# One weight load put behind four transposing DMAs, and twenty score products issued more than once, in a fused attention and MLP kernel

## Chip, cores and metric

The kernel runs on one core of a Trainium2 chip, as one launch. The metric is the device time of one execution in microseconds (us), from the median of the runs shown. Beside the timed runs stands one execution recorded by the hardware profiler.

## What is computed

The inputs are bf16: `x` of 2048 rows by 640, `wqkv` (640 x 1920), `wo` (640 x 640), and for the second branch `w1`, `w2` (640 x 640), `w3` (640 x 1536), `w4` (1536 x 640).

```python
def _A_ref(x, wqkv, wo):            # B=1, S=2048, D=640, H=32, Dh=20
    qkv = (x @ wqkv).reshape(B, S, 3, H, Dh).transpose(2, 0, 3, 1, 4)
    q, k, v = qkv[0], qkv[1], qkv[2]
    scores = jnp.einsum("bhqd,bhkd->bhqk", q, k) * (Dh ** -0.5)
    p = _softmax(scores, axis=-1)
    o = jnp.einsum("bhqk,bhkd->bhqd", p, v)
    return o.transpose(0, 2, 1, 3).reshape(B, S, D) @ wo

def _B_ref(x, w1, w2, w3, w4):
    h = _gelu(_layernorm(x) @ w1)
    # g0..g3: the four column quarters of h, shifted by +1, -1, +2, -2 rows
    x1 = x + jnp.concatenate([g0, g1, g2, g3], axis=-1) @ w2
    return x1 + _gelu(_layernorm(x1) @ w3) @ w4

xn = _layernorm(x)
return x + _A_ref(xn, wqkv, wo) * _silu(_B_ref(xn, w1, w2, w3, w4))
```

## The kernel before

The program is a list of tasks (`Task`), each with an engine, a function that issues its instructions, and the atoms it reads and writes. `Planner.follow` takes the tasks in the order of `TABLE`, a string in which each task stands as two characters (followed by one character for each buffer choice). This one order, written out, fixes the order on every engine and on SP's DMA queue; semaphores are derived from the atoms. An engine never overtakes its own order. A DMA task waits on SP for what it reads, and everything behind it on that queue waits with it.

**Prologue.** `load_inputs` brings `x` in eight loads. LayerNorm makes `xn`; `ln1_and_transpose` makes its transpose `xnT`, needed by all projections, in four groups `g` of 512 columns. Groups 0, 1 and 3 go through TensorE (transposes, line 1054) with evictions by VectorE (line 1065) or ScalarE (line 1062). Group 2 (`TD = (2,)`) goes through four transposing DMAs on SP, `tx_8` to `tx_11`, one for each 128 rows (line 1043). `prep` then makes the keys and queries of the first four heads: `KT_c` and `QT_c` are products of chunk `c` of `xnT` (`mm_tile`, line 708, five steps of four products each), so `KT_2` reads what the four DMAs write. Scores against the first keys and their exponentials begin while later key chunks are still being made.

In the SP order before, the load of W1 (`ld_w1`, lines 1937 and 1938, 640 x 640 bf16) stands after `tx_9` and before `tx_8`, `tx_10`, `tx_11`. Next behind these stands the copy of queries into `QM` (line 1365). W1 is first used by `b_w1`, which also multiplies by rows `RR` that SP loads later.

**Attention.** 32 heads in 8 quads of 4, each with 4 chunks `qc` of 512 queries and 16 key tiles `kt` of 128 keys. `score_pair(b, qc, kt, a, ...)` issues the products of two of the four heads (`a` = 0 or 1) for one key tile, into two PSUM banks. In one form (line 1594, `score`) it is two products, each on 32 rows of the array, 32 x 128 by 512 columns; the two pairs `a` use different rows. In the other (line 1607) it is eight products of 128 x 32. Which one is taken depends on the neighbours in the TensorE order (`mode`, set in `follow`). ScalarE takes the exponential of most pairs (`exp_act`, line 1654, 128 x 1024 in one instruction). For some pairs VectorE makes them from integer arithmetic instead: `score_both` (line 1685), then `block_bits` (line 1573 on VectorE, line 1571 on GpSimd). The products with V are lines 1407 and 1585.

**The second branch** is woven into the same order: `b_w1`, `b_w2`, `b_w3`, `b_w4` fill TensorE between scores; the last of it, the steps that end in line 2093 (tanh) and 2102, is done early in quad 7. After each chunk of quad 7, `finish_qc` multiplies with `wo` and stores.

Of the kernel before, what the change touches and what calls it, by code (L numbers as in the profile page):

```python
# [16 lines left out]


class Task:
    __slots__ = ("part", "flex", "id", "eng", "dur", "fn", "reads", "writes", "due", "name",  # L20
                 "preds", "succs", "order_preds", "start", "finish", "seq",
                 "signals", "dma_sem", "lat", "pos", "npred", "prio", "is_dma",
                 "acq", "rel", "stream", "sidx", "cls", "nbytes", "mode", "ndma", "tile", "dlat", "lock")
# [34 lines left out]
class Planner:  # L58
# [87 lines left out]
            self.buf_atoms[name].add(atom)  # L146

    def task(self, eng, dur, fn, reads=(), writes=(), due=None, name="", lat=0.0,
             is_dma=False, acq=None, rel=None, stream=None, after=(), cls=0, nbytes=0, mode=0, ndma=1, tile=None, dlat=0.0, lock=False, part=0, flex=False):
        tid = len(self.tasks)  # L150
        t = Task(tid, eng, dur, fn, tuple(reads), tuple(writes), due, name, lat, is_dma)
        t.cls = cls
        t.nbytes = nbytes
        t.mode = mode
        t.ndma = ndma
        t.tile = tile
        t.part = part or 3 * mode
        t.flex = flex
        t.dlat = dlat
        t.lock = lock or eng == "pool"  # L160
        if is_dma and nbytes:
            t.lat = self.dma_lat0 + nbytes / self.dma_bw + dlat
        t.acq = [acq] if isinstance(acq, tuple) else list(acq or ())
        t.rel = rel
        self.tasks.append(t)
        preds = set()
        opreds = set()
        for bn in after:
            preds.update(self.buf_inherit.get(bn, ()))
        if stream is not None:  # L170
            assert is_dma
            lst = self.streams.setdefault(stream, [])
            t.stream = stream
            t.sidx = ndma + (self.tasks[lst[-1]].sidx if lst else 0)
            if lst:
                preds.add(lst[-1])
            lst.append(tid)

        def add(p, atom):
            if p == tid:  # L180
                return
            pt = self.tasks[p]
            if (pt.eng == "pe" and eng == "pe" and atom in self.pe_psum_atoms
                    and not pt.is_dma):
                opreds.add(p)
            else:
                preds.add(p)

        for a in t.reads:
            own = self.atom_owner.get(a)  # L190
            if a in self.last_writer:
                add(self.last_writer[a], a)
            elif own is not None:
                for p in self.buf_inherit.get(own, ()):
                    add(p, a)
        for a in t.writes:
            own = self.atom_owner.get(a)
            seen = False
            if a in self.last_writer:
                add(self.last_writer[a], a)  # L200
                seen = True
            for r in self.readers.get(a, ()):
                add(r, a)
                seen = True
            if not seen and own is not None:
                for p in self.buf_inherit.get(own, ()):
                    add(p, a)
        for a in t.reads:
            self.readers[a].append(tid)
        for a in t.writes:  # L210
            self.last_writer[a] = tid
            self.readers[a] = []
        opreds -= preds
        t.preds = preds
        t.order_preds = opreds
        return t

    def follow(self, table):
# [19 lines left out]
        while at < len(table):  # L238
            t = tasks[len(code) * code[table[at]] + code[table[at + 1]]]
# [5 lines left out]
        while at < len(table):  # L245
            t = tasks[len(code) * code[table[at]] + code[table[at + 1]]]
            at += 2
            e = t.eng
            if e == "pe":
                nx = next(later)  # L250
                if t.flex and (pe_mode or (nx is not None and (nx.mode or nx.flex))):
                    t.mode, t.dur = 1, self.row_dur
            st = eng_free[e]
            if t.lock and e == "pool" and held_by is not None and held_by not in t.preds:
                t.preds.add(held_by)
# [217 lines left out]
class Cfg:  # L473
# [5 lines left out]
    def __init__(self, S=2048, D=640, H=32, F=1536):  # L479
# [93 lines left out]
        self.W7 = (0, 1)  # L573
        self.LAST = [[[4, 2]], [[3, 2]]]
        self.HP = True
        self.EARLY = 4
        self.PP |= {(quad, qc, 0, 2) for quad in range(8) for qc in range(4)}
        self.PP |= {(0, 0, 1, 3), (0, 0, 1, 2)}
# [59 lines left out]
class Gen:  # L638
# [29 lines left out]
    def A(self, name, *key):  # L668
        a = (name,) + key
        self.pl.own(name, a)  # L670
        return a
# [924 lines left out]
    def score_pair(self, b, qc, kt, a, hs, sa, gb):  # L1596
        T, A = self.T, self.A
        me = []
        early = self.tag == "0_0" and kt < self.cfg.EARLY
        def fn(e):  # L1600
            for jj in range(2):
                out = self.bank(hs[jj].slot if isinstance(hs, tuple) else hs.slots[jj])
                if me[0].mode:
                    ins = self.score(e, out[:, :], b, qc, kt, 2 * a + jj, early)
                    continue
                for c in range(4):
                    ins = e.matmul(out[32 * c:32 * c + 32, :], self.KT[:, b, 128 * kt + 32 * c:128 * kt + 32 * c + 32],  # L1607
                                   self.QM[:, gb, 2 * a + jj, :], start=True, stop=True, tile_position=(0, 32 * c))
            return ins
        me.append(T("pe", 220 if gb is None else 440, fn,  # L1610
                    reads=[A("KT", b, kt // 4)] + ([A("QE")] if early else [A("QT", b, qc), A("QTa", b, qc)]) + ([] if gb is None else [A("QM", gb)]),
                    writes=[sa], name=f"sc{self.tag}_{kt}_{a}", mode=int(gb is None), part=a + 1, flex=gb is not None, cls=-1,
                    acq=("S2",) + hs if isinstance(hs, tuple) else ("S", hs)))

    def score_act(self, b, qc, kt, a, gb=None):
# [289 lines left out]
    def b_alloc1(self):  # L1905

        cfg = self.cfg
        T, A = self.T, self.A
        S, D, KC, NT = cfg.S, cfg.D, cfg.KC, cfg.NT
# [24 lines left out]
          reads=[A("T16", 0), A("T16", 1)], writes=[("dq",)], is_dma=True, nbytes=8192, name="rr0", ndma=3)  # L1934
        self.RR = self.alloc("RR", [6, 512], FP32)
        W1 = self.W1 = self.alloc("W1", [KC, D], BF16)
        T("sp", C_SP, lambda e: e.dma_start(W1[:, :, :], self.aps["B_w1"].rearrange("(kc p) n -> p kc n", p=128)),
          writes=[A("W1")], is_dma=True, nbytes=KC * 128 * D * 2, name="ld_w1")
        W2 = self.W2 = self.alloc("W2", [KC, D], BF16)
        T("sp", C_SP, lambda e: e.dma_start(W2[:, :, :], self.aps["B_w2"].rearrange("(kc p) n -> p kc n", p=128)),  # L1940
          writes=[A("W2")], is_dma=True, nbytes=KC * 128 * D * 2, name="ld_w2")
# [171 lines left out]
    r"<%K&=&>%T&%O'%Z%[%P%Q$o'2(K%L*>$&?(T(L%U*<%M%t%V%W%]%_(%`%a%b%R%^'+#0&t%X%F%H%S%I&#)&$%c%N&%*3'*?#&&&'&*(&+&((M*4(*@)&,&-&.&/'?%'@'A'B'C&)&L$&C#&1*0#&2&6)&M&"  # L2113
# [115 lines left out]
```

## Time and profile before

| | |
|---|---|
| time, median of 3 runs | 797.91 us (797.26 to 798.15) |
| the profiled execution's own time | 799.57 us |
| its span, first to last instruction | 797.8 us |
| mean granted TensorE clock | 0.991 |
| busy: TensorE, ScalarE, VectorE, GpSimd | 774.4, 766.1, 688.1, 441.4 us |

In the profile PE is TensorE (PEld its weight loads), ACT ScalarE, DVE VectorE, POOL GpSimd, SP the engine that issues the DMAs. A row of the timeline has start, duration, engine, line, operation, what it writes and reads, how many instructions were merged, and in brackets the idle time before it and what ended it. Starts and ends of neighbouring instructions overlap, since the engines are pipelined. A row of the windows has the stretch, its length, and for each engine the busy time and the number of instructions, then the granted clock as a share of full speed, the DMA engines' mean busy share and their GB/s.

### The profile page before, as it was taken

How to read it: one execution, taken by the hardware profiler on the slowest of the kernel's cores; microseconds unless marked ns; L12 is line 12 of the kernel's file. 1: busy time of each engine (PE TensorE's matmuls, PEld its weight loads, DVE VectorE, ACT ScalarE, POOL GpSimd, SP SyncE). 2: the span in 40 equal slices, each digit the busy share in tenths (PEclk: the TensorE clock that was granted, in tenths of full speed). 3: DMA queues.
4: the chain of work that ended last, by engine and by line, in shares of the span. 5: the costliest groups of instructions: out<-in, count | busy, mean ns of one | idle time of the engine just before them, and what ended most of it. 6: DMA issues, size and time to landing. Idle time of an engine off the chain costs nothing.

```text
span 797.8 us, 29573 instructions
## 1 busy us (share of the span) xinstructions
PE 774.4 (97%) x13392; PEld 321.2 (40%) x13392; DVE 688.1 (86%) x914; ACT 766.1 (96%) x798; POOL 441.4 (55%) x238
## 2 busy tenths in 40 slices
PE   8899999999999999999999999999999999999996
PEld 5433333334444433333534444334334344433464
DVE  8788889989999999989998889898978888786876
ACT  7799999999999999999999999999999999998986
POOL 6476646552546647665653655756264464735832
PEclk9999999999999999999999999999999999997998
DMA  6421452342131322333241132324333113123353
GB/s 173 71 72 46 111 134 52 90 107 48 37 86 35 54 65 58 70 78 65 79 100 47 26 81 52 85 44 87 53 93 44 43 35 85 22 51 103 78 157 101
DMA packets 141357, 58.22 MB, mean 73 GB/s; under 512 B 113728, under 2 KB 136432, under 8 KB 141232
## 3 DMA queue, kind: packets, MB, share of 16 engines
q1 hardware_dynamic: 141232, 56.33, 31.2%
q8 instruction: 105, 1.72, 0.9%
q14 instruction: 20, 0.16, 0.1%
HBM read 34.70 MB, written 10.33 MB: 56 GB/s over the span
## 4 chain that ended last, share of the span: by engine, by line
ACT 54%; PE 36%; DVE 5%; DMA 3%; POOL 1%; issue 0%; SPq 0%; DVEq 0%
ACT arena L1654 47%; PE psum L708 13%; PE psum L1594 8%; PE psum L1585 6%; PE psum L1407 4%; PE psum L1607 4%; ACT arena L2065 3%; DVE arena L1685 2%; ACT arena L1636 1%; DMA arena<-arena 1%; ACT arena L1973 1%; ACT arena L2093 1%; DVE arena L1573 1%; PE psum L1464 1%; PE psum L1438 1%; POOL arena L1881 1%
## 5 line engine op out<-in xcount | busy, mean ns | idle before, releaser
L1654 ACT ACTIVATE arena<-psum 128x1024 bf16<-128x1024 f32 x726 | 678.3, 1038 | 18.7 <-PE psum L1594 14.0
L1571 POOL TENSOR_TENSOR arena<-arena 128x2048 int32<-128x2048 int32 x92 | 330.1, 3598 | 224.0 <-DVE arena L1573 104.4
L1685 DVE TENSOR_SCALAR arena<-psum 128x1024 uint16<-128x1024 f32 x268 | 326.3, 1220 | 55.1 <-PE psum L1594 49.8
L708 PE MATMUL psum<-arena 128*32 128x320 bf16 (+1 forms) x5808 | 336.0, 332 | 1.9 <-DMA arena<-arena 1.2
L1594 PE MATMUL psum<-arena 32*128 32x512 bf16 x1606 | 195.5, 387 | 10.7 <-ACT arena L1654 6.6
L708 PEld LDWEIGHTS psum<-arena 128*32 128x32 bf16 x5808 | 143.2, 96 | 122.0 <-issue 31.5
L1585 PE MATMUL psum<-arena 128*22 128x512 bf16 x2144 | 188.1, 383 | 0.0
L1407 PE MATMUL psum<-arena 128*22 128x512 bf16 x1448 | 137.8, 384 | 0.3
L1573 DVE TENSOR_SCALAR arena<-arena 128x4096 uint16<-128x4096 uint16 (+1 forms) x127 | 133.2, 1072 | 2.5 <-PE psum L1585 1.8
L1594 PEld LDWEIGHTS psum<-arena 32*128 32x128 bf16 x1606 | 53.6, 91 | 177.8 <-ACT arena L1654 97.7
L1607 PE MATMUL psum<-arena 128*32 128x512 bf16 x1512 | 114.9, 381 | 0.3
L1585 PEld LDWEIGHTS psum<-arena 128*22 128x22 bf16 x2144 | 52.5, 91 | 62.1 <-issue 26.1
L1720 POOL TENSOR_TENSOR arena<-arena 128x512 bf16<-128x512 f32 x30 | 40.8, 1360 | 27.1 <-DVE arena L1573 20.0
L1407 PEld LDWEIGHTS psum<-arena 128*22 128x22 bf16 x1448 | 35.7, 91 | 47.8 <-issue 22.8
L1607 PEld LDWEIGHTS psum<-arena 128*32 128x32 bf16 x1512 | 31.6, 95 | 40.9 <-ACT arena L1654 30.2
L2058 DVE CAST arena<-psum 128x512 bf16<-128x512 f32 x48 | 32.7, 682 | 4.5 <-PE psum L708 4.3
L1274 DVE CAST arena<-psum 128x512 bf16<-128x512 f32 x40 | 27.3, 687 | 8.2 <-PE psum L708 8.0
L1881 POOL TENSOR_TENSOR arena<-arena 128x640 bf16<-128x640 bf16 x12 | 16.7, 1398 | 23.4 <-DVE arena L1573 8.8
L919 DVE BATCH_NORM_STATS2 arena<-arena 128x6 f32<-128x320 bf16 x54 | 24.9, 482 | 0.6 <-DMA arena<-in_A_x_dram 0.5
L1636 ACT ACTIVATE arena<-psum 128x2048 bf16<-128x2048 f32 x13 | 24.7, 1897 | 0.7 <-PE psum L1594 0.7
L1819 DVE SCALAR_TENSOR_TENSOR arena<-psum,arena 128x320 bf16<-128x320 f32 x32 | 15.3, 484 | 11.1 <-PE psum L708 10.9
L1707 DVE STREAM_TRANSPOSE arena<-psum 128x512 f32<-128x512 f32 x30 | 21.3, 710 | 1.9 <-PE psum L1585 1.3
(133 smaller groups left out, 342.7 us busy)
## 6 DMA issues: line engine op xcount, KB each, us to landing
arena<-in_B_w_dram SPq DMA_DIRECT2D x48, 160.0 KB, 2.7
arena<-arena SPq DMA_DIRECT2D x124, 32.0 KB, 2.1
arena<-in_B_w_dram SPq DMA_DIRECT2D x4, 960.0 KB
arena<-in_A_x_dram SPq DMA_DIRECT2D x8, 320.0 KB, 5.7
arena<-in_A_x_dram SPq DMA_DIRECT2D x16, 160.0 KB, 2.5
out_dram<-arena SPq DMA_DIRECT2D x16, 160.0 KB, 2.3
heads<-arena SPq DMA_DIRECT2D x120, 20.0 KB, 2.0
arena<-keys SPq DMA_DIRECT2D x28, 80.0 KB
```

The source lines that it names most:

```text
L708: ins = e.matmul(pb[32 * c:32 * c + 32, 0:N], lhsT(k, c), rhs(k, c), start=(k == 0), stop=(stop and k == nk - 1), tile_position=(0, 32 * c))
L1407: ins = e.matmul(pb[32 * i:32 * i + 22, 0:512], VA[:, ql, kts[i // 2], i, :], PT[:, slots[i // 2][0].slot, 512 * (i % 2):512 * (i % 2) + 512],
L1571: return e.tensor_tensor(dst.bitcast(I32), U[:, ub, 0:w].bitcast(I32), bass.AP(c.tensor, c.offset, [list(c.ap[0]), [0, w // 2]]), op=ALU.add)
L1573: fa if onp else lambda e, v=v, dst=dst: e.tensor_scalar(dst, U[:, ub, 0:w], EXP_B[v], None, op0=ALU.add),
L1585: ins = e.matmul(pb[32 * i:32 * i + 22, 0:512], wv, dst[:, at:at + 512].bitcast(BF16), start=first, stop=final, tile_position=(0, 32 * i))
L1594: return e.matmul(out, self.KT[32 * i:32 * i + 32, b, 128 * kt:128 * kt + 128], q, start=True, stop=True, tile_position=(32 * i, 0))
L1607: ins = e.matmul(out[32 * c:32 * c + 32, :], self.KT[:, b, 128 * kt + 32 * c:128 * kt + 32 * c + 32], self.QM[:, gb, 2 * a + jj, :], start ...
L1636: lambda e: e.activation(self.PT[:, hp[0].slot:hp[0].slot + 2, :], self.psum[:, 512 * h0.slot:512 * h0.slot + 2048].rearrange("p (a b) -> ...
L1654: lambda e: e.activation(self.PT[:, hp.slot, :], self.psum[:, 512 * hs.slot:512 * hs.slot + 1024], AF.Exp, scale=cfg.scale),
L1685: ins = e.tensor_scalar(U[:, ub, 1024 * at + 512 * k:1024 * at + 512 * k + w], self.psum[:, 512 * hd.slots[k]:512 * hd.slots[k] + w], a_ex ...
L1720: return e.tensor_tensor(OnT.rearrange("p (k d a) -> p a k d", k=4, a=4), Ob[:, :].rearrange("p (a k d) -> p a k d", a=4, k=4), in1, op=AL ...
L2058: T("dve", c_dve(512), lambda e, h=h, fc=fc, i=i, G=G: e.tensor_copy(G[:, i, fc, :], self.wbank(h)[:, 0:512]), reads=[wa], writes=at, name ...
```

## The change

Two edits.

First, the task `ld_w1` now reads the four atoms that the transposing DMAs write, so SP issues it only when all four have landed, and its place in `TABLE` (the two characters `(T`) moves from after `tx_9` to after `tx_11` (`%I`).

Second, a table `AGAIN` names fourteen score pairs by (quad, qc, kt, a) and how many more times each is issued, 20 times together. The pair's products go into the same banks again with the same operands, each starting anew, so the values stay; the pair's semaphore comes with the last product. The order of the tasks does not change. All fourteen pairs are of the form of line 1594, two products each.

```diff
+        self.AGAIN = {(2, 2, 5, 0): 1, (2, 2, 7, 1): 1, (2, 3, 4, 0): 1, (3, 1, 7, 1): 1, (6, 1, 3, 0): 1, (6, 1, 6, 1): 1, (7, 1, 0, 0): 3, (7, 1, 0, 1): 1, (7, 1, 2, 0): 3, (7, 1, 5, 0): 1, (7, 1, 5, 1): 1, (7, 1, 6, 0): 1, (7, 1, 10, 0): 2, (7, 1, 15, 0): 2}
...
     def score_pair(self, b, qc, kt, a, hs, sa, gb):
         T, A = self.T, self.A
         me = []
+        quad = int(self.tag.split("_")[0])
         early = self.tag == "0_0" and kt < self.cfg.EARLY
+        times = 1 + self.cfg.AGAIN.get((quad, qc, kt, a), 0)
         def fn(e):
-            for jj in range(2):
+            for jj in list(range(2)) * times:
                 out = self.bank(hs[jj].slot if isinstance(hs, tuple) else hs.slots[jj])
...
         T("sp", C_SP, lambda e: e.dma_start(W1[:, :, :], self.aps["B_w1"].rearrange("(kc p) n -> p kc n", p=128)),
-          writes=[A("W1")], is_dma=True, nbytes=KC * 128 * D * 2, name="ld_w1")
+          reads=[A("xnT", "t", g, bi) for g in cfg.TD for bi in range(4)], writes=[A("W1")], is_dma=True, nbytes=KC * 128 * D * 2, name="ld_w1")
...
-    ...&?(T(L%U*<%M%t%V%W%]%_(%`%a%b%R%^'+#0&t%X%F%H%S%I&#)...
+    ...&?(L%U*<%M%t%V%W%]%_(%`%a%b%R%^'+#0&t%X%F%H%S%I(T&#)...
```

The other lines pass `times` through to the task, where `follow` lets the modelled duration of the pair grow with it.

More of the change, by code (lines that the diff above doesn't have):

```diff
@@ L19 @@
 class Task:
-    __slots__ = ("part", "flex", "id", "eng", "dur", "fn", "reads", "writes", "due", "name",
+    __slots__ = ("part", "times", "flex", "id", "eng", "dur", "fn", "reads", "writes", "due", "name",
                  "preds", "succs", "order_preds", "start", "finish", "seq",
@@ L148, in task @@
     def task(self, eng, dur, fn, reads=(), writes=(), due=None, name="", lat=0.0,
-             is_dma=False, acq=None, rel=None, stream=None, after=(), cls=0, nbytes=0, mode=0, ndma=1, tile=None, dlat=0.0, lock=False, part=0, flex=False):
+             is_dma=False, acq=None, rel=None, stream=None, after=(), cls=0, nbytes=0, mode=0, ndma=1, tile=None, dlat=0.0, lock=False, part=0, flex=False, times=1):
         tid = len(self.tasks)
@@ L158, in task @@
         t.flex = flex
+        t.times = times
         t.dlat = dlat
@@ L251, in follow @@
                 if t.flex and (pe_mode or (nx is not None and (nx.mode or nx.flex))):
-                    t.mode, t.dur = 1, self.row_dur
+                    t.mode, t.dur = 1, self.row_dur * t.times
             st = eng_free[e]
@@ L1609, in fn @@
             return ins
-        me.append(T("pe", 220 if gb is None else 440, fn,
+        me.append(T("pe", (220 if gb is None else 440) * times, fn,
                     reads=[A("KT", b, kt // 4)] + ([A("QE")] if early else [A("QT", b, qc), A("QTa", b, qc)]) + ([] if gb is None else [A("QM", gb)]),
-                    writes=[sa], name=f"sc{self.tag}_{kt}_{a}", mode=int(gb is None), part=a + 1, flex=gb is not None, cls=-1,
+                    writes=[sa], name=f"sc{self.tag}_{kt}_{a}", mode=int(gb is None), part=a + 1, flex=gb is not None, cls=-1, times=times,
                     acq=("S2",) + hs if isinstance(hs, tuple) else ("S", hs)))
@@ L2112 @@
     r"E&p%v($C%6&q&c&d%;&r%x#',$'-$I'.%y%w$J&e$K*:#$g$h*.$%G&s$A%z$L$i'/%{%|'0&{%*;)$j$B$k&|&}&~*5#*/%'1%}#/$l'#*6&'%$'&'''(')*=$&_#5'$$m$M%~'**8#$n&:%&;%Y#*9'%J$&"
-    r"<%K&=&>%T&%O'%Z%[%P%Q$o'2(K%L*>$&?(T(L%U*<%M%t%V%W%]%_(%`%a%b%R%^'+#0&t%X%F%H%S%I&#)&$%c%N&%*3'*?#&&&'&*(&+&((M*4(*@)&,&-&.&/'?%'@'A'B'C&)&L$&C#&1*0#&2&6)&M&"
+    r"<%K&=&>%T&%O'%Z%[%P%Q$o'2(K%L*>$&?(L%U*<%M%t%V%W%]%_(%`%a%b%R%^'+#0&t%X%F%H%S%I(T&#)&$%c%N&%*3'*?#&&&'&*(&+&((M*4(*@)&,&-&.&/'?%'@'A'B'C&)&L$&C#&1*0#&2&6)&M&"
     r"N&O'D&P&0&D&@&7&Q*D$*1'*E#*F#*2&E*G*R(&F*S%&G&8(*7*n#*I(&9*o'&H*M&*A'M('N*K'O*N$'P'Q*H#&A%*B*J)(N&u$&v&w'R&B*O&*C*P&'E'3(&x'4&y&z*v#*L'5'6*w('7'8*T&*X(*l#'9("
```

## The prediction

> **What bounds the kernel now.** I read the page first: busy times, the forty slices, the chain, the group with the most busy time.
>
> ```profile
> span 797.8 us, 29573 instructions
> ...
> PE 774.4 (97%) x13392; PEld 321.2 (40%) x13392; DVE 688.1 (86%) x914; ACT 766.1 (96%) x798; POOL 441.4 (55%) x238
> ...
> ACT  7799999999999999999999999999999999998986
> ...
> PEclk9999999999999999999999999999999999997998
> ...
> ACT 54%; PE 36%; DVE 5%; DMA 3%; POOL 1%; issue 0%; SPq 0%; DVEq 0%
> ...
> L1654 ACT ACTIVATE arena<-psum 128x1024 bf16<-128x1024 f32 x726 | 678.3, 1038 | 18.7 <-PE psum L1594 14.0
> ```
>
> The exponentials on ScalarE (line 1654) set the pace, with TensorE close behind; 54% of the chain is ACT, 36% PE. ACT is idle for only 797.8 - 766.1 = 31.7 us. The slices say where: the first two, and those near slice 36, where the granted clock of TensorE is also below full. A microsecond that ACT loses in such a place is paid at the end, because ACT is full afterwards. So the change is worth what ACT gets back in two places: the prologue and the stretch around 720 us. I then asked for the timeline of each and for the windows of 3.41 us around the second.
>
> **Part one: the load of W1 goes behind the transposes.** In the SP queue before, the load of W1 (line 1937) stands between the first and the other three transposing DMAs (line 1043) that make columns 1024 to 1535 of `xnT`.
>
> ```profile
> 17.68 2.70 SPq L1043 DMA_TRANSPOSE arena<-arena  x1
> 20.43 0.57 SPq L1937 DMA_DIRECT2D arena<-in_B_w_dram  x1
> 21.05 4.66 SPq L1043 DMA_TRANSPOSE arena<-arena  x3
> 43.77 3.34 SPq L1365 DMA_DIRECT2D arena<-arena  x4
> ```
> ```profile
> L1043 SPq DMA_TRANSPOSE arena<-arena x4: 1222/1674/2697, 17.7 to 23.6; - x4
> ...
> DMA to landing us min/median/max: 3.8/6.3/7.1
> ```
> ```profile
> GB/s 0 0 0 0 47 45 205 121 6 9 83 0 0 66 44 22 84 234 322 380 399 388 370 268 178 241 99 1 8 10 135 231 286 51 0 0 47 0 0 0
> ```
>
> The last line is 17 to 31 us in 40 slices of 0.35 us: W1 flows at 234 to 399 GB/s from about 23 to 25 us, and what moves at 25 to 27 and 27.5 to 29 is the rest of the transposes, with a hole between. ACT and PE pay for it here:
>
> ```profile
> 27.20 0.60 ACT L1062 ACTIVATE arena<-psum 128x512 bf16<-128x512 bf16 x1 [0.27 <-PE psum L1054]
> ...
> 28.37 0.41 PE L1054 MATMUL psum<-arena 128*32 128x128 bf16 x16 [1.15 <-issue]
> ...
> 29.94 0.83 PE L708 MATMUL psum<-arena 128*32 128x512 bf16 x12 [1.16 <-DMA arena<-arena]
> ...
> 30.70 0.40 PE L1594 MATMUL psum<-arena 32*128 32x512 bf16 x4
> ...
> 31.13 1.94 ACT L1654 ACTIVATE arena<-psum 128x1024 bf16<-128x1024 f32 x2 [3.33 <-PE psum L1594]
> ```
>
> TensorE stops twice. At 29.94 it waits 1.16 us for the transposes (the key products of chunk 2). Before 28.37 it stands still for 1.15 us with no wait in sight, just while the DMA line is at 1 to 10 GB/s. I read that as its own instructions arriving late through the same blocked DMA engines, which is an inference. ACT, free at 27.80, gets its next scores at 31.13: 3.33 us idle.
>
> With the change the last three transposes move up by W1's slot of 0.62 us: the first of them at 20.43, the last, two spacings of (23.6 - 21.05)/2 = 1.3 later, at 23.0. By the shortest landing, 3.8 us, it is there at 26.8; by the median, 6.3, at 29.3. The 3.8 is nearer, since the longer ones had W1 ahead of them. TensorE is out of other work at 28.37 - 1.15 = 27.22. Upper bound: both holes vanish and the score products come 30.70 - 29.94 = 0.76 after 27.22, the exponential 31.13 - 30.70 = 0.43 later, at 28.41: 2.72 us gained. Without the transposes' share, 29.3 instead of 29.94: 0.6. Below that, nothing: if the transposes are slow by themselves, W1's absence changes nothing. A loss needs W1 to be missed: it would be issued at about 27 and, if it takes its 5.6 us (the row shown last below), be there before 33. I take 2.4, next to the two holes' 2.31.
>
> The moved load now waits for all four transposes on SP. Behind it on that queue stands only the copy at 43.77, which has 16 us to spare, and all of the RR rows that W1's products also read come after that copy, so W1 isn't needed before. Nothing is moved past another engine's queue.
>
> ```profile
> arena<-in_B_w_dram SPq DMA_DIRECT2D x1, 800.0 KB, 5.6
> ```
>
> **Part two: repeated score products.** Fourteen of the twenty belong to quad 7, chunk 1; counted in program order they lie between 715 and 725 us. The stretch in windows (PE, PEld, DVE, ACT, POOL busy, granted clock, DMA, GB/s):
>
> ```profile
> 25.59:29.01 3.42, 2.04 (x88) 1.27 (x80) 1.46 (x4) 1.93 (x3) 2.50 (x7) 1.00 1.09 112
> ...
> 296.97:300.38 3.41, 3.11 (x33) 0.87 (x32) 3.40 (x5) 3.36 (x5) 3.03 (x1) 1.00 0.52 166
> ...
> 715.09:718.50 3.41, 2.39 (x24) 0.49 (x18) 3.19 (x3) 3.41 (x4) 0.33 (x1) 1.00 0.75 246
> 718.50:721.91 3.41, 2.64 (x12) 0.51 (x12) 2.75 (x4) 3.07 (x5) 2.75 (x1) 0.50 0.41 71
> 721.91:725.33 3.42, 3.36 (x28) 0.64 (x28) 1.41 (x2) 2.62 (x4) 3.42 (x2) 0.50 0.66 219
> 725.33:728.74 3.41, 3.41 (x32) 0.78 (x28) 0.49 (x1) 2.46 (x4) 0.98 (x1) 0.50 0.67 203
> ```
>
> The clock is halved for exactly three such windows, 718.50 to 728.74, right behind one with 24 products. The rest of the body keeps its clock, also at 296.97 with 33. So few products, not a long pause, bring the drop: the longest hole in the row below is 0.57. [...]
>
> ```profile
> 714.88 0.60 PE L1594 MATMUL psum<-arena 32*128 32x512 bf16 x6 [0.28 <-ACT arena L1654]
> 715.42 0.40 PE L1585 MATMUL psum<-arena 128*22 128x512 bf16 x4
> 715.64 0.39 PE L1407 MATMUL psum<-arena 128*22 128x512 bf16 x4
> 716.60 0.74 PE L1594 MATMUL psum<-arena 32*128 32x512 bf16 x4 [0.57 <-DVE arena L1685]
> 717.27 0.40 PE L1585 MATMUL psum<-arena 128*22 128x512 bf16 x4
> 717.86 0.39 PE L1594 MATMUL psum<-arena 32*128 32x512 bf16 x2 [0.20 <-ACT arena L1654]
> 718.78 0.61 PE L1594 MATMUL psum<-arena 32*128 32x512 bf16 x2 [0.53 <-ACT arena L1654]
> ...
> 722.51 0.61 PE L1585 MATMUL psum<-arena 128*22 128x512 bf16 x4
> 722.90 0.64 PE L1407 MATMUL psum<-arena 128*22 128x512 bf16 x4
> ```
> ```profile
> 715.81 3.83 ACT L1654 ACTIVATE arena<-psum 128x1024 bf16<-128x1024 f32 x4
> 719.98 3.77 ACT L1654 ACTIVATE arena<-psum 128x1024 bf16<-128x1024 f32 x4 [0.34 <-PE psum L1407]
> 724.55 1.94 ACT L1654 ACTIVATE arena<-psum 128x1024 bf16<-128x1024 f32 x2 [0.80 <-PE psum L1594]
> 727.07 1.02 ACT L1654 ACTIVATE arena<-psum 128x1024 bf16<-128x1024 f32 x1 [0.58 <-PE psum L1594]
> 728.47 1.02 ACT L1654 ACTIVATE arena<-psum 128x1024 bf16<-128x1024 f32 x1 [0.38 <-PE psum L1407]
> ```
>
> A round costs 715.64 - 715.42 = 0.22 us at full clock and about 0.40 at half (722.51 to 722.90). Price of the drop: ACT's four stalls, 0.34 + 0.80 + 0.58 + 0.38 = 2.10, and each also loses the overlap of neighbouring exponentials, 1.04 alone against (3.83 - 1.04)/3 = 0.93 in a row, 4 x 0.11 = 0.44. Together 2.54. If the clock holds, ACT itself is what is late next.
>
> The repeats add 0.22 each. Three more in the row of 714.88 (0.66) push the next two rounds to an end of 715.86 + 0.66 = 716.52, before 716.60: hidden. From 716.60 to the next pair at 718.78 are 2.18 us, with two pairs, one round and one pair in them, 4 x 0.22 = 0.88; two repeats at the end of the row of 716.60 and three in that of 717.86 add 5 x 0.22 = 1.10, which makes 1.98: it fits. None of these eight delays an exponential: the two after 715.81 start a pitch of 0.93 apart from full buffers, and the third at 719.98 waits for line 1407. The other six of the stretch cost 6 x 0.22 = 1.3 at most and nothing at least; I take 0.3, since several of their consumers do wait on the score. The six elsewhere (quads 2, 3 and 6) cost 0 to 6 x 0.22 = 1.3: the window of 296.97 has 0.30 of PE idle and ACT full, so hidden in part; 0.3. If PE had no holes there, all 1.3 would be paid. With eight repeats of two products, the window of 715.09 goes from 24 products to about 40: above the 33 that kept the clock.
>
> **Sum.** 2.4 + 2.54 - 0.3 - 0.3 = 4.3 us. The profiled execution took 799.57 (1.77 around its span): it would take 795.2. The median shown, 797.91, is 1.66 lower; I take the same difference off it: 793.6.
>
> **Rivals.**
> - *The hole without a wait stays* (TensorE is starved by the transposes alone): part one gives 1.2, the rest as before: 794.8. For it: the profile names no releaser. 0.15.
> - *The timed runs have a shorter drop than the profiled one.* [...] As a mechanism of this kernel: the median lies 1.66 below the profile, and if all of that were clock, part two gains 0.9 instead of 2.54: 795.2; if there were none at all, 797.91 - 2.4 + 0.6 = 796.1. [...] 0.09.
> - *The drop stays in its place.* Then 2.54 isn't gained and the six repeats after 718.50 cost 0.40 each, 2.4, less some 1 us of holes: 797.91 - 2.4 + 0.3 + 1.4 = 797.2, no change. 0.09.
> - *Slower: the drop comes one window earlier and is paid by all fourteen.* Decided by whether about 40 products, most of them 32*128 and so on a quarter of the rows, count as enough activity. 14 x 0.40 = 5.6, holes of about 2.1 cover part: 3.5, plus 0.3, less part one's 2.4: 1.4 more, and up to 3 if part one gives its 0.6: 799.3 to 801. 0.05.
>
> **How the numbers follow.** The forecast has 0.62. A measurement of this kernel can tell about 0.2%, 1.6 us, so faster means below 796.3: forecast, first and second rival, 0.86; same 0.09; slower 0.05. The range: the best case of both parts, 2.72 + 2.54 = 5.3, and a little more for repeats that cost less than nothing in a warm stretch, gives 792.3; the upper end at 796.1 takes in the second rival and the forecast with part one at 0.6. Outside lie the last two, 0.14, and some of the tails.
>
> **What would show it.** Right: SP issues the four transposes in a row and W1 after they have landed, near 27; ACT's idle before its first exponential after 28 falls from 3.33 to about 0.6, PE's two holes of 1.15 and 1.16 are gone; the granted clock is 1.00 in all slices but the last; ACT's four stalls between 719 and 729 go; there are 20 x 2 = 40 more products of line 1594's kind. Wrong: a clock of 0.50 anywhere in the body, an unexplained PE hole near 26 to 28 us that remains, or ACT stalls of 0.2 each in quads 2, 3 and 6.

## The result, and the profile after

| | before | after |
|---|---|---|
| median, 6 runs each on the same chip | 797.63 us (797.23 to 800.1) | 794.59 us (794.06 to 795.49) |
| the profiled execution, its span | 799.57 us, 797.8 | 794.99 us, 793.2 |
| mean granted clock in it | 0.991 | 0.998 |

The ratio is 0.9958 (95% interval 0.9944 to 0.9972): 3.0 us faster, by the interval 2.2 to 4.5. One execution of a kernel below (W1 alone) took 1270.22 us at a mean clock of 0.6, and its median is that of the other eleven. The page after, for the rows shown of before:

```profile
span 793.2 us, 29655 instructions
...
PE 773.7 (98%) x13432; PEld 321.6 (41%) x13432; DVE 688.2 (87%) x914; ACT 765.9 (97%) x798; POOL 441.5 (56%) x238
...
ACT  7899999999999999999999999999999999999996
...
PEclk9999999999999999999999999999999999999999
...
ACT 56%; PE 37%; DVE 4%; DMA 1%; issue 0%; SPq 0%; DVEq 0%
...
L1658 ACT ACTIVATE arena<-psum 128x1024 bf16<-128x1024 f32 x726 | 678.3, 1038 | 14.3 <-PE psum L1596 11.0
```

ScalarE is busy as long as before (765.9 against 766.1 us); what is gone is its idle time: 793.2 - 765.9 = 27.3 instead of 31.7, of that 4.4 in the group of exponentials (18.7 to 14.3). The clock row has no slice below 9. There are 13432 - 13392 = 40 products more.

**The prologue.** The timeline after, SP first, then TensorE and ScalarE; behind them the landing of the transposing DMAs and the DMA line for 17 to 31 us in slices of 0.35 us:

```profile
17.68 8.07 SPq L1045 DMA_TRANSPOSE arena<-arena  x4
27.92 0.39 SPq L1941 DMA_DIRECT2D arena<-in_B_w_dram  x1
41.78 3.33 SPq L1367 DMA_DIRECT2D arena<-arena  x4
...
27.25 0.70 PE L1056 MATMUL psum<-arena 128*32 128x128 bf16 x36
27.95 0.83 PE L710 MATMUL psum<-arena 128*32 128x512 bf16 x12
28.71 0.40 PE L1596 MATMUL psum<-arena 32*128 32x512 bf16 x4
27.71 0.60 ACT L1064 ACTIVATE arena<-psum 128x512 bf16<-128x512 bf16 x1 [0.27 <-PE psum L1056]
29.14 1.94 ACT L1658 ACTIVATE arena<-psum 128x1024 bf16<-128x1024 f32 x2 [0.83 <-PE psum L1596]
```
```profile
DMA to landing us min/median/max: 3.5/4.2/4.4
```
```profile
GB/s 0 0 0 0 0 47 217 235 8 90 146 10 10 169 53 0 0 0 117 208 91 1 8 10 83 176 195 117 0 0 0 47 0 0 73 59 51 194 322 380
```

The four transposes go out in a row, land after 4.2 us in the median (6.3 before), and only then, at 27.92, W1 is issued: its 322 and 380 GB/s now stand at the end of the line. TensorE's rows at 27.25 and 27.95 have no bracket: both holes are gone. ACT's gap ahead of its first exponential fell from 3.33 to 0.83 us, and that exponential starts at 29.14 instead of 31.13.

**The stretch of the drop.** In the profile of before the granted clock changes at 718.50, 728.74 and 793.59 us, the last time when TensorE's work runs out: 10.24 and 64.85 us apart, 3 and 19 times 3.413. So I count windows of 3.413 us back from the last change, which is at 790.56 in the profile after. These are they (columns as in the prediction: PE, PEld, DVE, ACT, POOL, clock, DMA share, GB/s; an instruction on a border counts on both sides), and the exponentials behind them:

```profile
712.06:715.47 3.41, 3.13 (x54) 1.21 (x50) 2.82 (x4) 3.41 (x4) 0.95 (x1) 1.00 0.39 81
715.47:718.89 3.42, 3.22 (x34) 0.95 (x30) 3.28 (x3) 3.42 (x5) 0.92 (x1) 1.00 0.94 273
718.89:722.30 3.41, 2.80 (x36) 0.82 (x34) 2.16 (x4) 3.41 (x5) 3.41 (x2) 1.00 0.16 38
722.30:725.71 3.41, 3.38 (x56) 1.31 (x60) 1.04 (x1) 3.27 (x4) 2.82 (x1) 1.00 0.74 233
```
```profile
714.62 11.47 ACT L1658 ACTIVATE arena<-psum 128x1024 bf16<-128x1024 f32 x12
725.98 1.27 ACT L2097 ACTIVATE arena<-arena 128x1280 bf16<-128x1280 bf16 x1
```

No window has a clock of 0.50, and twelve exponentials run without a pause where before four stalls of 0.34 to 0.80 us stood between them.

**Where the 4.53 us between the two profiles came from.** I laid the starts of the same exponentials beside each other; the last of them starts 4.53 us earlier than before. The prologue gives 1.99. The stretch from 710 to 735 us gives 2.43. Small losses near 270, 515 and 626 us take 0.35 + 0.30 + 0.15 back. The last 0.94 comes after 745 us, where the change has done nothing: 0.73 of it in the chain of DMAs behind the last chunks. The timelines of SP, before and after:

```profile
745.22 1.24 SPq L1729 DMA_TRANSPOSE arena<-arena  x1
749.50 2.59 SPq L1742 DMA_DIRECT2D heads<-arena  x4
```
```profile
741.92 1.24 SPq L1733 DMA_TRANSPOSE arena<-arena  x1
744.62 2.58 SPq L1746 DMA_DIRECT2D heads<-arena  x4
```

From a transposing DMA to the copies that wait for it passed 4.28 us before and 2.70 after. The kernels below have this 0.73 as well, W1 alone among them and also the one with W1's burden doubled, which has neither part of the change, and one more profile of the kernel before has 0.25 of it: the first profile of before was an unlucky one there, and this is no term of the change.

### The profile page after: what moved, and what is told of

The parts are those of the page before. It is cut to its first block, busy times and chain, and to the rows that moved or that the text cites. A ratio compares the mean times of both kernels' runs of the same rounds, so it can differ in the third digit from the quotient of the medians.

```text
span 793.2 us, 29655 instructions
## 1 busy us (share of the span) xinstructions
PE 773.7 (98%) x13432; PEld 321.6 (41%) x13432; DVE 688.2 (87%) x914; ACT 765.9 (97%) x798; POOL 441.5 (56%) x238
## 4 chain that ended last, share of the span: by engine, by line
ACT 56%; PE 37%; DVE 4%; DMA 1%; issue 0%; SPq 0%; DVEq 0%
ACT arena L1658 49%; PE psum L710 14%; PE psum L1596 8%; PE psum L1587 5%; PE psum L1409 4%; PE psum L1611 3%; ACT arena L2069 3%; DVE arena L1689 2%; ACT arena L1640 2%; ACT arena L1977 1%; ACT arena L2097 1%; PE psum L1466 1%; DMA arena<-arena 1%; PE psum L1440 1%; ACT L1658 0%; DVE arena L921 0%
## 5 line engine op out<-in xcount | busy, mean ns | idle before, releaser
L1658 ACT ACTIVATE arena<-psum 128x1024 bf16<-128x1024 f32 x726 | 678.3, 1038 | 14.3 <-PE psum L1596 11.0
L1724 POOL TENSOR_TENSOR arena<-arena 128x512 bf16<-128x512 f32 x30 | 40.8, 1362 | 27.3 <-DVE arena L1575 20.0
L1611 PEld LDWEIGHTS psum<-arena 128*32 128x32 bf16 x1512 | 31.7, 95 | 40.8 <-ACT arena L1658 30.1
L1276 DVE CAST arena<-psum 128x512 bf16<-128x512 f32 x40 | 27.3, 687 | 8.0 <-PE psum L710 7.8
```

Source lines behind the costliest of these rows:

```text
L1658: lambda e: e.activation(self.PT[:, hp.slot, :], self.psum[:, 512 * hs.slot:512 * hs.slot + 1024], AF.Exp, scale=cfg.scale),
L1724: return e.tensor_tensor(OnT.rearrange("p (k d a) -> p a k d", k=4, a=4), Ob[:, :].rearrange("p (a k d) -> p a k d", a=4, k=4), in1, op=AL ...
```

## The experiments

The theory: part one removes ScalarE's wait for key chunk 2, part two keeps one window of the granted clock from being thin; the two add up. The rivals: only the one or the other counts; the six repeats outside quad 7 are needed as well; the repeats themselves cost time; or the order matters less than the wait that ld_w1 got.

**W1 alone.** No pair is issued more than once.

```diff
-        self.AGAIN = {(2, 2, 5, 0): 1, (2, 2, 7, 1): 1, ... (7, 1, 15, 0): 2}
+        self.AGAIN = {}
```


> W1 behind the transposes, no score product repeated. My theory (two separate gains): TensorE's two holes before the key products of chunk 2, 2.3 us together, are gone, and the drop of the clock to 0.50 near 718 us (before: 718.50 to 728.74) is still there. 2.0 to 2.5 us less than before in the profile, so about half of the change's 3.0 in the medians; 795.4 or so if before is at 797.6. Rival (the clock alone does it, the prologue is given back later): no difference from before, within 0.3 us. Rival (W1 does all of it): the full 3 us, 794.6, and the clock then doesn't matter.

Measured: a median of 796.8 us (795.06 to 798.92, 11 runs) against 797.82; ratio 0.998 (0.996 to 1.0). Its first exponential in the prologue, and the windows around the drop:

```profile
28.55 1.94 ACT L1658 ACTIVATE arena<-psum 128x1024 bf16<-128x1024 f32 x2 [0.74 <-PE psum L1596]
```
```profile
712.72:716.13 3.41, 2.32 (x24) 0.49 (x18) 3.26 (x3) 3.41 (x5) 0.25 (x1) 1.00 0.83 259
716.13:719.54 3.41, 2.65 (x14) 0.53 (x14) 2.74 (x4) 3.08 (x5) 2.83 (x1) 0.50 0.37 59
719.54:722.95 3.41, 3.41 (x28) 0.62 (x28) 1.40 (x2) 2.61 (x3) 3.41 (x2) 0.50 0.67 228
```

The prologue's gain is there in full (28.55 against 31.13 in the first profile of before). The drop is there too, behind a window with 24 products, as before; here it lasts two windows instead of three. The two parts are separate. In medians part one is worth 1.0, where I had expected about 2.2, and the interval of this run alone can't tell 1.0 from 2.4, nor from nothing.

**The repeats alone.** All twenty repeats; W1 back in its old place, without the reads.

```diff
-          reads=[A("xnT", "t", g, bi) for g in cfg.TD for bi in range(4)], writes=[A("W1")], ..., name="ld_w1")
+          writes=[A("W1")], ..., name="ld_w1")
-    ...&?(L%U*<%M%t%V%W%]%_(%`%a%b%R%^'+#0&t%X%F%H%S%I(T&#)...
+    ...&?(T(L%U*<%M%t%V%W%]%_(%`%a%b%R%^'+#0&t%X%F%H%S%I&#)...
```


> All 20 repeats, W1 at its old place in the queue. My theory: granted clock 1.00 up to 790 us, ACT without the four stalls of 0.34 to 0.80 near 720; the holes of 1.15 and 1.16 in the prologue stay. The repeats themselves cost 0.4 to 0.6 in quads 2, 3 and 6. Net 0.5 to 2 us less than before by how long the drop is in the runs of before. Rival (the repeats are pure cost, the drop costs nothing at the end because DMA takes over): 0.5 us more than before.

Measured: 795.84 (794.72 to 798.37, 12 runs), ratio 0.997 (0.9953 to 0.9988); the mean clock is 0.995 to 0.999. The prologue in its timeline:

```profile
27.48 0.41 PE L1056 MATMUL psum<-arena 128*32 128x128 bf16 x16 [0.64 <-issue]
...
28.81 0.83 PE L710 MATMUL psum<-arena 128*32 128x512 bf16 x12 [0.92 <-DMA arena<-arena]
...
30.00 1.94 ACT L1658 ACTIVATE arena<-psum 128x1024 bf16<-128x1024 f32 x2 [2.58 <-PE psum L1596]
```

Both holes are there with W1 ahead, but as 0.64 and 0.92 us: 1.56 together, not the 2.31 of the profile from which part one was priced. Part two works without part one and is worth 797.82 - 795.84 = 2.0. Three of the twelve runs, at mean clocks of 0.995 and 0.996, took 797.57 to 798.37; the other nine, at 0.997 to 0.999, 794.72 to 795.98. Where these three lost clock no profile shows. A drop in the prologue, as the second profile of before has it below, would fit: then W1's old place costs not only its holes but, in some executions, a drop that they set off.

**W1 and the fourteen repeats of quad 7**, without the six elsewhere.

```diff
-        self.AGAIN = {(2, 2, 5, 0): 1, (2, 2, 7, 1): 1, (2, 3, 4, 0): 1, (3, 1, 7, 1): 1, (6, 1, 3, 0): 1, (6, 1, 6, 1): 1, (7, 1, 0, 0): 3, ...
+        self.AGAIN = {(7, 1, 0, 0): 3, ...
```


> The change without the six repeats in quads 2, 3 and 6 (the fourteen in quad 7 stay). My theory: no drop anywhere, since those places held their clock before; the 0.35 us that the exponentials fall back near 270 us and the 0.15 near 626 in the changed kernel aren't lost: 0.5 us less than the changed kernel, 794.1 or so. Rival (the six keep the clock up in some phases of the windows): some of the runs show a clock lower by 0.004 or more and are 1 to 3 us longer.

Measured: 794.45 (793.47 to 796.52, 12 runs), ratio 0.995 (0.9933 to 0.9967); the mean clock is 0.997 to 0.999 in all runs. That can't be told from the changed kernel's 794.59, measured on another chip; the 0.5 us less that I had expected did not come. The six neither help nor cost what can be measured; between the profiles they take 0.15 us, at quad 6, in both kernels that have them. On the same chip, this kernel less W1 alone is 794.45 - 796.8 = -2.35, which is the repeats of quad 7; this kernel less the repeats alone is 794.45 - 795.84 = -1.39, which is W1's place beside the repeats (less the six elsewhere, some 0.15). Resampling the runs gives these two differences 95% intervals of 0.6 to 4.1 and 0.8 to 2.5 (an estimate from 11 or 12 runs each).

**W1's burden doubled.** The kernel before, with the load of W2, also 800 KB, put on SP's queue right behind that of W1, ahead of the three transposes.

```diff
-    ...&?(T(L%U*<%M...        # tx_9, ld_w1, tx_8, ...
+    ...&?(T(U(L%U*<%M...      # tx_9, ld_w1, ld_w2, tx_8, ...
```


> The kernel before, with the load of W2 (as large as W1, 0.82 MB) right behind W1 and so also ahead of the three transposes: the suspected cost doubled. My theory (the transposes' packets queue behind the weights' packets): W1 took about 2.2 us of the DMA engines, so TensorE's wait for the transposes grows by about 2 us, from 1.16 to 3.2, and the time by 2 us. Rival (the hole is the fetch of TensorE's instructions stalling with the transposes, whatever is ahead): the wait changes by less than 0.5 us, the time too.

Measured: 803.04 (801.03 to 805.67, 8 runs), ratio 1.006 (1.0036 to 1.0084): 5.2 us slower, against some 2 expected. The two holes and the windows of the prologue:

```profile
29.40 0.41 PE L1054 MATMUL psum<-arena 128*32 128x128 bf16 x16 [1.95 <-issue]
...
31.17 1.47 PE L708 MATMUL psum<-arena 128*32 128x512 bf16 x12 [1.37 <-DMA arena<-arena]
```
```profile
27.59:31.00 3.41, 0.41 (x16) 0.23 (x16) 1.29 (x4) 0.44 (x1) 0.84 (x4) 1.00 0.62 98
31.00:34.41 3.41, 3.24 (x32) 0.89 (x36) 0.19 (x1) 1.19 (x2) 0.00 (x0) 0.50 0.02 5
```

The wait for the transposes, which was to grow to 3.2, hardly grew (1.16 to 1.37), and so both the theory and its rival were half wrong: what grew is the hole without a named wait, from 1.15 to 1.95. As the prediction inferred, this hole is longer with more load ahead on the DMA engines: 0.64, 0.85 and 1.15 us in three profiles with W1 ahead of the transposes, 1.95 with W1 and W2, and none where W1 stands behind them (the changed kernel, W1 alone, the order without the wait).

The DMA packets in the traces hint at what TensorE lacked there. Queue q8 carries packets of 16,384 bytes that the profile marks as instructions, 105 of them in the profile of before and as many in that after:

```profile
q8 instruction: 105, 1.72, 0.9%
```

Over TensorE's 26,784 products and weight loads in the profile of before that is 64.2 bytes for each, so I take them for TensorE's instructions, some 255 in a packet; this is an estimate from these numbers, and the profile does not name their engine. The two profiles have four stalls of TensorE over 0.2 us without a named wait: before, 0.36 us up to 13.72 and 1.15 up to 28.37; after, 0.49 up to 13.72 and 0.27 up to 18.24. They end 1.45, 1.59, 1.45 and 1.49 us after the end of such a packet, and stand behind 447, 1213, 447 and 701 of TensorE's instructions, that is 254 and 512 apart (a record can be missing). The hole of part one is the one behind 1213. With W1 ahead, the packet before it, the fourth of the execution, ends at 26.78 us; in the changed kernel the fourth ends at 24.68, and the hole is gone. I read this as TensorE waiting in the hole for its next packet of instructions, which came later with W1 ahead; the traces show the times, not the reason.

Then comes what I had not expected: the holes leave one window with 16 products, and the next one has half the clock. By the starts of the exponentials this profile loses 2.5 us against the first profile of before up to 40 us, and 1.2 near 520 us, where TensorE waits for a slice of W3 (line 2053):

```profile
519.48 0.61 PE L708 MATMUL psum<-arena 128*32 128x512 bf16 x8 [1.30 <-DMA arena<-in_B_w_dram]
```

Four other profiles have this wait too (0.36 to 1.04 us), all with W1 behind the transposes and the changed kernel's among them, so it isn't due to W2's place. Profile against profile the doubled load costs 3.4 us (802.98 against 799.57); what makes it 5.2 in the medians isn't shown. Here the loads ahead of the transposes cost twice: by the holes of 1.95 and 1.37 us, and by the clock of 0.50 in the window behind them.

**The kernel before once more**, without an edit, for a second profile.

> The kernel before, once more, for a second profile of it. My theory (the first profile of before was an unlucky one): TensorE's two holes between 27 and 30 us, 1.15 and 1.16, come out smaller, 0.5 to 2.0 together, since a kernel with W1 at its old place showed only half of them; the drop near 718 us is there, with 6.8 or 10.2 us at clock 0.50; the chain of DMAs between 745 and 760 us gives back the 0.73 us that all four changed kernels have there. Rival (the profile was a typical one): holes of 2.3 within 0.2, the same 0.73.

Measured: 800.05 us, span 798.3, clock 0.992.

```profile
28.57 0.41 PE L1054 MATMUL psum<-arena 128*32 128x128 bf16 x16 [0.85 <-issue]
...
29.92 0.83 PE L708 MATMUL psum<-arena 128*32 128x512 bf16 x12 [0.94 <-DMA arena<-arena]
```
```profile
27.74:31.15 3.41, 1.64 (x36) 0.69 (x40) 1.41 (x4) 0.59 (x2) 0.94 (x4) 1.00 0.30 64
31.15:34.56 3.41, 3.41 (x40) 1.49 (x36) 1.20 (x3) 2.57 (x3) 0.00 (x0) 0.50 0.00 0
...
717.23:720.64 3.41, 2.31 (x24) 0.49 (x18) 3.27 (x3) 3.41 (x5) 0.24 (x1) 1.00 0.81 256
720.64:724.05 3.41, 2.66 (x14) 0.54 (x14) 2.74 (x4) 3.07 (x5) 2.84 (x1) 0.50 0.38 61
```

The holes are smaller than in the first profile (1.79 together), and the late drop is 6.8 us long, not 10.24. But this execution has a drop in the prologue as well, which costs 1.67 us by the starts of the exponentials between 31.1 and 36.8 us. The windows do not begin at the same place in each execution: in the prologue they begin at 25.59 in the first profile and at 27.74 in this one, where the work is only 0.5 us apart. They cut the thin stretch of the prologue differently: the window of 25.59 has 88 products and keeps the clock, the one of 27.74 has 36 and is followed by half of it. The starts of the late drop (718.50, 720.64, and 716.13 with W1 alone) are no sign of this: laid against the exponentials, these three stand at the same place in the work within 0.1 us. The kernel before scatters from 795.28 to 802.49 in 71 runs over three sessions, and its time goes, by and large, with the mean clock: on average 801.9 at 0.986, 800.7 at 0.990, 798.8 at 0.992, 797.1 at 0.994, but also 799.9 at 0.988. That the phase of the windows is what scatters it would fit this, but no run sets the phase.

**The first eight repeats, or the last six.** W1 in its new place; of quad 7 only the repeats before 718 us, or only those behind.

```diff
# first eight
+        self.AGAIN = {(7, 1, 2, 0): 3, (7, 1, 10, 0): 2, (7, 1, 0, 0): 3}
# last six
+        self.AGAIN = {(7, 1, 6, 0): 1, (7, 1, 15, 0): 2, (7, 1, 5, 1): 1, (7, 1, 5, 0): 1, (7, 1, 0, 1): 1}
```


> W1 moved, and of the repeats only the first eight in quad 7 (key tiles 2, 10 and 0, pair 0). My theory (the count of products in a window of 3.41 us decides, between 24 and 33): the window that was the first thin one is now full, but the following stretch has only some 14 products in a window, so the clock still drops in most runs, a window later: clock 0.992 to 0.995, 1 to 2.5 us more than with all fourteen (794.5). Rival (filling the first thin window is enough): clock 0.998 in all runs, 794.5.

> W1 moved, and of the repeats only the last six in quad 7 (key tiles 6, 15, 5, and pair 1 of tile 0). My theory: the first thin window still has 24 products or fewer, the drop comes at the same place as without repeats, and the six are paid at half clock: 797 to 798, no better than W1 alone (796.8). Rival (only the length of the thin stretch counts, and what is left of it is under two windows): a drop in half of the runs at most, median 795.5 or less.

Measured: the first eight 794.97 (794.33 to 795.11, 6 runs), ratio 0.9941 (0.9926 to 0.9957); the last six 796.03 (794.86 to 799.54, 12 runs), ratio 0.9971 (0.9956 to 0.9986), both against 798.91. The windows, of the first eight and of the last six:

```profile
715.30:718.72 3.42, 2.95 (x28) 0.90 (x26) 3.28 (x3) 3.42 (x4) 1.20 (x1) 1.00 0.88 248
718.72:722.13 3.41, 2.38 (x28) 0.77 (x32) 2.38 (x4) 3.41 (x5) 3.41 (x2) 1.00 0.18 54
```
```profile
715.49:718.90 3.41, 2.11 (x20) 0.57 (x16) 3.27 (x4) 3.41 (x5) 0.23 (x1) 1.00 1.08 304
718.90:722.31 3.41, 3.21 (x27) 0.78 (x27) 2.19 (x3) 2.89 (x4) 3.41 (x2) 0.50 0.14 17
722.31:725.73 3.42, 3.42 (x34) 0.67 (x26) 1.71 (x2) 2.61 (x4) 3.42 (x1) 0.50 0.73 226
```

I had expected the first eight alone to move the drop one window later and to leave 1 to 2.5 us on the table; that fell. Filling the first thin stretch is almost enough. In three of the six runs the mean clock is 0.994 or 0.995, so there it still drops somewhere; the one profile, at 0.999, does not show where. Those three take 794.97 to 795.05, and the other three 794.33 to 795.11: wherever that drop is, it costs under 0.8. The last six alone leave the window of 715.49 with 20 products, and the next two are halved. Their clock is 0.990 to 0.996 in all twelve runs, and they are 1.5 us slower than all fourteen in the same session (794.56, below). The 797 to 798 that I had expected was too high; W1 alone was not run in that session, so whether the last six gain anything beside it isn't shown.

**Three repeats once each.** W1 in its new place, and one repeat for each of the three pairs of the first eight.

```diff
+        self.AGAIN = {(7, 1, 2, 0): 1, (7, 1, 10, 0): 1, (7, 1, 0, 0): 1}
```


> W1 moved, and in quad 7 only three repeats, one each for key tiles 2, 10 and 0 (pair 0). By the run with eight, filling the first thin window was enough. My theory now (the count in a window decides, between 24 and 33 products): 24 + 6 = 30 is near the bound, so the clock drops in some of the runs and not in others, by the phase of the windows: 795 to 796. Rival (eight were needed): a drop in every run, 796.8 as with W1 alone. Rival (any break in the thin stretch is enough): no early drop, 794.5 to 795.

Measured: 796.29 (794.37 to 797.4, 12 runs) against 798.8, ratio 0.997 (0.9958 to 0.9982). All twelve runs have a mean clock of 0.990 to 0.995.

```profile
712.78:716.20 3.42, 2.89 (x30) 0.53 (x22) 3.33 (x3) 3.42 (x5) 0.19 (x1) 1.00 0.83 264
716.20:719.61 3.41, 2.14 (x18) 0.68 (x22) 3.18 (x4) 3.41 (x5) 2.90 (x1) 1.00 0.36 53
719.61:723.02 3.41, 3.41 (x30) 0.60 (x22) 1.32 (x2) 2.97 (x4) 3.41 (x2) 0.50 0.69 221
```

I had expected the phase to spare some of the runs and 795 to 796; by their clocks none was spared, and the rival, that more than three are needed, was nearer. The window with 30 products kept the clock, the next one with 18 lost it. Three repeats fill one window, and the thin stretch is two windows long.

**Order without the wait.** W1 stands behind `tx_11` but no longer reads what the transposes write; the repeats of quad 7 alone.

```diff
-          reads=[A("xnT", "t", g, bi) for g in cfg.TD for bi in range(4)], writes=[A("W1")], ..., name="ld_w1")
+          writes=[A("W1")], ..., name="ld_w1")
```


> W1 behind the transposes in the queue, but without the wait for them; fourteen repeats in quad 7. My theory (W1 only has to stand behind them): the same time as with the wait, 794.5 within 0.3, and no hole. Rival (the wait is needed, since the weights' packets overtake or crowd the transposes' when both are in flight): TensorE waits 0.5 us or more for the transposes, 795 or more.

Measured: 794.56 (794.13 to 795.66, 6 runs), ratio 0.9939 (0.9922 to 0.9956).

```profile
25.11 0.59 SPq L1941 DMA_DIRECT2D arena<-in_B_w_dram  x1
...
27.12 0.83 PE L710 MATMUL psum<-arena 128*32 128x512 bf16 x12
...
28.31 1.94 ACT L1658 ACTIVATE arena<-psum 128x1024 bf16<-128x1024 f32 x2 [0.80 <-PE psum L1596]
```

W1 goes out 2.8 us earlier than in the changed kernel, while the transposes are still in flight, and no hole appears. The place behind the transposes is what counts. The wait adds nothing, and as nothing else needs the queue then, it costs nothing.

**Twenty repeats where TensorE is full.** W1 and the repeats of quad 7, and twenty pairs between 442 and 480 us once more each.

```diff
-        self.AGAIN = {(2, 2, 5, 0): 1, ... (6, 1, 6, 1): 1, (7, 1, 0, 0): 3, ... (7, 1, 15, 0): 2}
+        self.AGAIN = {(7, 1, 0, 0): 3, ... (7, 1, 15, 0): 2, (4, 1, 10, 1): 1, ... (4, 3, 6, 0): 1}   # 20 of quad 4
```


> W1 moved, the fourteen repeats in quad 7, and twenty further pairs issued once more, but between 442 and 478 us, where TensorE has no hole (busy 36.00 of 36.00 us in before). My theory (a repeat is free only where TensorE waits): each is paid with 0.22 us as far as ACT has to wait for the scores behind it; ACT itself is busy 35.86 of 36.00 there, so most of 20 x 0.22 = 4.4 us, at least 2, comes on top of 794.5: 796.5 to 799. Rival (TensorE's busy share overstates it and ACT's pace hides the repeats): 0.5 us or less on top.

Measured: 797.59 (796.99 to 798.87, 12 runs) against 798.8, ratio 0.999 (0.9976 to 1.0004): 3.1 us more than the 794.5 without them, which was measured in two other sessions; against the before of each session it is 2.2 to 3.1. The stretch, in this kernel and in the kernel before:

```profile
442.00:480.00 38.00, 38.00 (x706) 16.07 (x706) 30.81 (x40) 35.97 (x37) 18.79 (x7) 1.00 0.29 51
```
```profile
442.00:478.00 36.00, 36.00 (x696) 16.20 (x688) 30.70 (x40) 35.86 (x40) 20.29 (x7) 1.00 0.28 56
```

TensorE is busy without a gap there. By the starts of the exponentials the stretch grows by 3.79 us, 0.19 for each repeat, close to the 0.22 that a round costs. Here a repeat was not free where TensorE has no holes; that the repeats of the change cost next to nothing fits the holes in which they stand.

## Why the prediction was right, and where a size was off

The forecast was 793.6 and the result is 794.59; faster came out, and the forecast lies inside the interval. The forecast of the profiled execution, 795.2, met 794.99, but partly by luck: the 0.94 us after 745 us, which is no term of the change, made up for the 0.8 lost near 270, 515 and 626 us and for a prologue that gave 1.99 instead of 2.4.

- **Part one, the mechanism.** Right, and shown: both holes are gone, and the gap of 3.33 became 0.83. The exponential was to start at 28.41 at best; it came at 29.14; 0.51 us of that were lost before 22 us, where this profile has a stall of TensorE near 18 us that other profiles have elsewhere or not at all. The first rival (the hole without a wait stays) fell: it is gone in the changed kernel, with W1 alone and in the order without the wait, and grew from 1.15 to 1.95 us when W2 joined W1. The inference of instructions arriving late fits the packets on q8 (the fourth ends at 26.78 us before, at 24.68 after), but no run shows that TensorE waits for them. Of the wait for the transposes, 0.21 us is left in one profile (the twenty repeats where TensorE is full).
- **Part one, the size.** This is the term that was mis-sized. 2.4 is what one profile showed. With W1 ahead the two holes were 2.31, 1.79 and 1.56 us in three profiles, and in medians the place of W1 is worth 1.39 (beside the repeats) or 1.0 (without). One profile of before is one draw from a kernel that scatters by 7 us.
- **Part two.** Right in mechanism: 2.54 less 0.3 was forecast for quad 7. The profile gave 2.43, and the medians 2.35 beside W1's new place and 2.0 beside the old one, with all twenty. But the size depends on the drop that is removed. The first profile of before had one of 10.24 us; with the 6.8 us drop of W1 alone, profile against profile, the fourteen repeats gain only 1.2 us. That the eight earliest repeats decide, by filling the window of 24 products to about 40, holds in part: the window has 34, the first eight alone get nearly all, and the last six alone don't hold the clock. The price of the last six, 0.3, and of the six elsewhere, 0.3, was on the high side: nothing that a median shows, 0.15 in profiles for the latter. That no long pause is needed for the drop holds: the longest pause of TensorE in the two windows before the drop of before was 0.57 us. The number of products alone does not decide: 28 kept the clock and 36 lost it (last section).
- **From the profile to the median.** The step "1.66 lower; I take the same difference off" took the profile's excess for something that the change leaves alone; the changed kernel's profile lies only 0.40 above its median (794.99 against 794.59). Part of the excess lay in just the places that the change mends: a drop of 10.24 us where other executions had 6.8, and holes of 2.31 where others had 1.6 to 1.8. These terms should have been made smaller first. The gain measured is 3.0 in the changed kernel's own comparison, 3.4 and 4.35 by nearly the same kernels in two other sessions, since the median of before itself was 797.63, 797.82 and 798.91; between these nothing here decides.
- **The other rivals.** A shorter drop in the timed runs is what happened in part: of the four profiles without repeats in quad 7 two have a late drop of 10.24 us and two one of 6.8, which is worth 1.2 with W1 alone. It did not eat the gain of 2.35 in the medians, so other runs of W1 alone must lose more than its profile does; their clocks go from 0.988 to 0.994. The drop in its place, and the one a window earlier, appeared in no run of the changed kernel: all six have clocks of 0.997 or 0.998.

## What to carry to other kernels

Look at a drop of the granted clock by the windows that its changes mark: here a thin window of 24 products stood ahead of it, the drop was gone with 34 products there, and a few products issued again in the holes of that window were cheaper than the drop, as long as TensorE really had holes there. A load that nobody needs soon goes behind the transfers for which an engine waits; here its place on the queue was enough (794.56 us without a wait, 794.45 with it). Before pricing a change from one profile, compare its stalls with a second profile of the same kernel, and shrink the terms that were larger in the first.

## What the runs showed of the hardware

- TensorE stood still without any wait on record for 1.15, 0.85, 0.64 and 1.95 us in the prologue when weight loads were ahead of the transposing DMAs (before, before once more, the repeats alone, the two loads), and not there when they were behind (the changed kernel, W1 alone, the order without the wait). In the profiles of before and after, its four stalls of this kind ended 1.45 to 1.59 us after the end of a packet of 16,384 bytes marked as instructions and stood 254 or 512 of its instructions apart.
- A long pause was not needed for half the clock: the longest in the two windows before the drop of before was 0.57 us. Products in the window ahead of a drop in the prologue or near 718 us: 24 (before, before once more, W1 alone), 20 (the last six), 18 (three repeats once) and 16 (the two loads), and 36 in one case (the prologue of before once more), 16 of them of 128 columns only. Neither the number of products nor PE's busy time separates the windows: 28 products with 2.38 us kept the clock (the first eight's window of 718.72), as did 88 with 2.04 us (before, 25.59), and 24 with 2.39 us lost it (before, 715.09).
- In the profiles of before and after, the columns of the products do separate the windows. I counted by the shapes in the profile, with 512 for each 128x512 or 32x512, 320 for each 128x320 and 128 for each 128x128, shared out by time where a product crosses a border. The three windows at full clock that were followed by half the clock have some 11,200 columns (715.09, before), 7,400 and 5,100 (the last before the end of each profile), and the 456 that were followed by full clock have 14,500 or more. In the drop of before the first two windows have 6,100 and 11,900, and the one after which it ended 12,700. This was found in the traces afterwards; no run was made to test it, and records of products can be missing.
- The windows did not begin at the same place in two executions of one kernel: those of the prologue at 25.59 and at 27.74 us, where the work was 0.5 us apart.
- The drops near 718 us lasted one, two or three windows: 3.41 us (three repeats once), 6.8 (W1 alone, before once more, the last six) and 10.24 (before).
